# One gradient stored feature-major and turned on its way back, normalised rows turned by SyncE instead of TensorE, layer 2 scheduled later

## The chip, the cores and the metric

The kernel runs on one core of a Trainium2 chip. The metric is the device time of one execution in microseconds (us), as the median of several runs. The engines are named as the profile names them: PE (TensorE, matmuls), DVE (VectorE), ACT (ScalarE), POOL (GpSimd) and SP (SyncE, which here only issues DMAs).

## What is computed

A forward pass of four blocks over x (2048 rows, D = 448 features) and the gradient of its result with respect to eight inputs. Block A is a gated long convolution, block B a two-layer perceptron with F = 1792 hidden features; both are used twice with the same weights.

```
def A(q, k, v, shift_k, ssm_k, ssm_D):
    kv = shift_conv(k, shift_k) * v
    y = causal_conv(kv, ssm_k) + kv * ssm_D        # by FFT of length 4096
    return q * y
def B(x, w1, w2):
    return silu(x @ w1) @ w2
x = A_q
x = x + A(layernorm(x), ...)
x = x + B(layernorm(x), w1, w2)                    # layer 1
x = x + A(layernorm(x), ...)
x = x + B(layernorm(x), w1, w2)                    # layer 2
out, vjp = jax.vjp(all of it);  grads = vjp(grad_out)
```

y does not depend on x, so it is computed once. The gradients of w1 and w2 sum over all 2048 rows and both layers.

## The kernel before, in words

The program has three stages. `Head` computes y by FFT matmuls into the SBUF tile Y. `Flow` then works through 16 tiles of 128 rows. `Tail` computes the weight gradients (its jobs "w2" and "w1") and, by another FFT, the gradients of block A's inputs.

**Order.** Nothing is issued in the order of the source. Every step is a call of `s.op` with an estimated cost for each engine that may do it, the tiles that it reads and writes, and a priority `prio` (smaller is earlier; one unit is about one us). `Sched.plan` plays the steps through with these costs and writes an order for each engine: an engine that is free takes the ready step with the smallest priority for which buffers are free (`_slots`, ring sizes in `BUFS`). `RATE` gives its DMA rates in bytes per us. `emit` then issues the steps in that order. On the chip each engine works strictly in order, and semaphores do the rest.

**A tile** (`Flow.tile(j)`, base priority `b = 20 j`; layer 2 at `c = b + 20`, the gradient of layer 1 at `d = c + 20`):

- x0 is normalised (`norm`: statistics on DVE, a power on POOL, the scaling on DVE), gated (`gate`), giving x1, and normalised again, giving n1.
- n1 must be feature-major for the up-projection. `turn` does four 128x128 transposes on PE into PSUM (L627) and one copy to SBUF, the tile nT, on DVE or ACT (L92, L94).
- `up` (L645, L654, L655) multiplies w1 by nT into two PSUM tiles; `silu` (L673) makes aT and the derivative dT of them on ACT. The two functions need different tables; `TURNED` lists where the derivative comes first.
- `down` (L689) multiplies aT by w2. x2, n2, x3 and n3 follow, then the same for layer 2.
- Backwards, grad_out's tile g is turned by two DMA transposes that SP issues (L757, L758). `grad_up` gives ghT of layer 2 (gh2), `back` and `gate_back` give the tile G2. G2 is turned by `turn` like n1 and n3, and gives gh1 and the gradient of q.

So three turns are done on PE for each tile, 48 in all.

**Stores for the weight gradients.** a1, a2, gh2 and gh1 are feature-major (128 features x 14 x 128 rows); the weight gradients need them row-major. `store_turned` (L676 to L681) has SP issue a DMA transpose into the SBUF tile `turned` (three buffers) and then a plain DMA of it to DRAM: A_d[0], A_d[1], GH_d[1] and GH_d[0]. In `Tail.jobs`, `bring` (L1067 to L1073) loads 256 features of all 16 tiles (1 MB) into a buffer `jb`: three in a ring, and for some loads of "w1" a spare one in the place of Minv, once Minv has been read. PE multiplies `jb` by gmov, G2 or nmov (L1124). The last tile's part of A_d[1] is taken from `turned` itself (`k.lastA`).

Of the kernel before, what the change touches and what calls it, by code (L numbers as in the profile page):

```python
# [13 lines left out]
BF16 = mybir.dt.bfloat16  # L14
ACT = mybir.ActivationFunctionType
ALU = mybir.AluOpType
# [4 lines left out]
P = 128  # L21
S = 2048
D = 448
F = 1792
J = 16
# [107 lines left out]
class Sched:  # L133
# [3 lines left out]
    AHEAD = 0.2  # L137
    STEP = 20
    RATE = {"plain": 300e3, "turn": 160e3}
# [99 lines left out]
    def plan(self):  # L239
# [4 lines left out]
        dma_free = 0.0  # L244
# [103 lines left out]
class Head:  # L348
# [11 lines left out]
    def run(self, pr):  # L360
# [52 lines left out]
        for b in range(4):  # L413
            n = 128 if b < 3 else 64
            for g in range(2):
                pt = s.vb("ps", "d", [P, 8, n], BF16, "ps_kt")

                def tk(e, b=b, g=g, pt=pt, n=n):
                    kv = ksb[b][:].rearrange("p (n1 n2) -> p n2 n1", n2=16)
                    for i in range(8):  # L420
                        nc.tensor.transpose(pt[:, i, :], kv[:, 8 * g + i, :], k.ident[:n, :n])

                s.op({"PE": 0.88}, tk, r=[ksb[b]], w=[pt], prio=pr + 0.1 * b)
                c = n / 128
                s.op({"DVE": 0.07 + 0.54 * c, "ACT": 0.08 + 0.82 * c}, lambda e, b=b, g=g, pt=pt, n=n: _copy(nc, e, kt()[:, 8 * g:8 * g + 8, 128 * b:128 * b + n], pt[:]), r=[pt], w=[kts[b][g]], prio=pr)
# [4 lines left out]
        for jq in range(4):  # L430
            for h in range(2):
                pt = s.vb("ps", "d", [DC, 2, 4, P], BF16, "ps_kT")

                def tt(e, jq=jq, h=h, pt=pt):
                    for u in range(4):
                        for c in range(2):
                            lo = (2 * h + c) * DC
                            nc.tensor.transpose(pt[:, c, u, :], Y.t[:, 4 * jq + u, lo:lo + DC], k.ident[:])

                s.op({"PE": 0.45}, tt, r=k.Yv[4 * jq:4 * jq + 4], w=[pt], prio=pr + 0.2)  # L440
                s.op({"DVE": 0.61, "ACT": 0.9}, lambda e, jq=jq, h=h, pt=pt: _copy(nc, e, kT[h]()[:, jq, :, :, 1:129], pt[:]), r=[pt], w=[kTs[h][jq]], prio=pr + 0.2)
# [3 lines left out]
        for n2 in (*range(1, 16), 0):  # L445
            ps = self.unit([P, 2, 512], name="ps_s1")

            def s1(e, n2=n2, ps=ps):
                for c in range(2):
                    nc.tensor.matmul(ps[:, c, :D], lhsT=M1[:, n2, c, :], rhs=kt()[:, n2, :], start=True, stop=True)  # L450

            s.op({"PE": 0.38}, s1, r=[m1s[n2 // 8], *[x[n2 // 8] for x in kts]], w=[ps], prio=pr, hold=[A1K])
            s.op({"ACT": 0.8, "DVE": 1.0}, lambda e, n2=n2, ps=ps: _copy(nc, e, A1K[:, :, :, n2, :].rearrange("p dh c ds -> p c dh ds"), ps[:, :, :D].rearrange("p c (dh ds) -> p c dh ds", ds=4)),
                 r=[ps], w=[aks[n2]], prio=pr)
# [29 lines left out]
        for ci in range(NCI):  # L484
            turn(A1K, [A1K], Z, zs, ci, pr + 2 + 0.1 * ci)
        for ci in range(NCI):
            stage2(Z, zs, ci, pr + 2 + 0.1 * ci)
# [58 lines left out]
        for h in range(2):  # L546
            for i, jq in enumerate((1, 2, 3, 0)):
                conv(h, jq, pr + 2 + 0.1 * (2 * (4 * h + i)))
# [9 lines left out]
            for ci in range(7 * h, 7 * h + 7):  # L558
                turn(A1v, [avs[ci]], X, xs, ci, pr + 4 + 0.1 * ci - 0.3)
            for ci in range(7 * h, 7 * h + 7):  # L560
                chunk(ci, pr + 4 + 0.1 * ci)
# [4 lines left out]
        for i in range(8):  # L566
# [7 lines left out]
            q = -6 + 0.1 * i if i else -20  # L574
# [5 lines left out]
T_ = 20.0  # L580
EARLY = 2
ROWS = (0, 128, 256, 320)
TURNED = ((1, 0), (1, 1), (3, 0))


class Flow:
# [89 lines left out]
    def store_turned(self, src, dst, j, pr):  # L676
        nc, s = self.nc, self.s
        an = self.small("turned", (P, NF, P))
        self.k.last_turn_out = s.op({"SP": 2.2}, lambda e: nc.sync.dma_start_transpose(out=an[:], in_=src[:].rearrange("p a s -> p (a s)")), r=[src], w=[an], prio=pr, dma=("turn", 458e3))
        s.op({"SP": 0.4}, lambda e: nc.sync.dma_start(out=dst[:, j, :], in_=an[:].rearrange("p a f -> p (a f)")), r=[an], w=[self.k.st_[(id(dst), j)]], prio=pr + 3, dma=("plain", 458e3))  # L680
        return an  # L681
# [42 lines left out]
    def tile(self, j):  # L724
        nc, s, k = self.nc, self.s, self.k
        b = T_ * j
        y = k.Yv[j]
# [7 lines left out]
        self.norm(x0, n0, rs[0], b - 14)  # L735
        self.gate(x0, n0, y, x1, b - 10)
        self.norm(x1, n1, rs[1], b - 8)
        s.op({"POOL": 0.6}, lambda e: nc.gpsimd.dma_start(out=_pm(k.N_d[0][:])[:, j, :], in_=n1[:]), r=[n1], w=[k.st_[("n", 0, j)]], prio=b + 10, dma=("plain", 115e3))
        a1, s1 = self.silu(self.turn(n1, b - 3, "nT1"), 0, b, (j, 0) in TURNED)
        self.store_turned(a1, k.A_d[0], j, b + 4)  # L740
        po = self.down(a1, k.w2, "ps_o", b + 8.6)
        x2, n2, x3, n3 = self.small("x2"), self.small("n2"), self.small("x3"), self.small("n3")
        s.op({"DVE": 0.64}, lambda e: nc.vector.tensor_tensor(out=x2[:], in0=x1[:], in1=po[:, :D], op=ALU.add), r=[x1, po], w=[x2], prio=b + 11)
        self.norm(x2, n2, rs[2], b + 12)
        self.gate(x2, n2, y, x3, b + 16)
        self.norm(x3, n3, rs[3], b + 18)
        s.op({"POOL": 0.6}, lambda e: nc.gpsimd.dma_start(out=_pm(k.N_d[1][:])[:, j, :], in_=n3[:]), r=[n3], w=[k.st_[("n", 1, j)]], prio=b + 35, dma=("plain", 115e3))
        c = b + T_
        a2, s2 = self.silu(self.turn(n3, c + 2.7, "nT3"), 1, c + 5.6, (j, 1) not in TURNED)
        up2 = self.last_up  # L750
        k.lastA = self.store_turned(a2, k.A_d[1], j, c + 10)
        k.lastA_op = k.last_turn_out
# [4 lines left out]
        s.op({"SP": 0.7}, lambda e: nc.sync.dma_start_transpose(out=gT[:, 0:3, :], in_=g[:, 0:384]), r=[g], w=[gT], prio=c - 4, dma=("turn", 98e3))  # L757
        s.op({"SP": 0.4}, lambda e: nc.sync.dma_start_transpose(out=gT[:, 3, :], in_=g[:, 320:448]), r=[g], w=[gT], prio=c - 4, dma=("turn", 33e3))  # L758
        gh2 = self.grad_up(gT, s2, c + 11.3, [up2])
        k.lastG = self.last_up  # L760
        self.store_turned(gh2, k.GH_d[1], j, c + 15)
        po2 = self.down(a2, k.w2, "ps_o", c + 14.2)
# [5 lines left out]
        self.back(gh2, n3, rs[3], g, G3, c + 19.8)  # L768
        s.op({"DVE": 0.32}, lambda e: nc.vector.tensor_tensor(out=gy2[:], in0=G3[:], in1=n2[:], op=ALU.mult), r=[G3, n2], w=[gy2], prio=c + 30)
        self.gate_back(G3, rs[2], y, n2, G2, c + 25)  # L770
# [4 lines left out]
        self.back(gh1, n1, rs[1], G2, G1, d + T_ + 3)  # L775
        gy = self.small("gy")
        q = d + T_ + 8
# [5 lines left out]
    def back(self, gh, n, r, res, out, pr):  # L783
# [4 lines left out]
        s.op({"ACT": 0.85}, lambda e: nc.scalar.activation(u[:], pn[:, :D], ACT.Identity, scale=r[:], accum_out=cp[:, 0:1]), r=[pn, r], w=[u, cp], prio=pr + 3)  # L788
        self.norm_back(u, n, cp, res, out, pr + 4)
# [8 lines left out]
class Tail:  # L798
# [242 lines left out]
    def jobs(self, which, pr):  # L1041
        nc, s, k = self.nc, self.s, self.k
        if which == "w2":
# [4 lines left out]
            groups = [(k.A_d[1], [gs[t // 4] for t in range(NT)], lambda t: gm[:, t, :]), (k.A_d[0], k.G2v, lambda t: k.G2[:, t, :])]  # L1048
        else:
# [7 lines left out]
            groups = [(k.GH_d[1], [nh[1][t // 8] for t in range(NT)], lambda t: nm[1][:, t, :]), (k.GH_d[0], [nh[0][t // 8] for t in range(NT)], lambda t: nm[0][:, t, :])]  # L1057
# [9 lines left out]
        def bring(p, gi, lo, hi, at=None):  # L1067
            b, part, spare = fetch(p, gi, which == "w1" and (2 * p + gi) % 4 == 0)
            src = groups[gi][0]
            v = b.sub()  # L1070
            part[lo:hi] = [v] * (hi - lo)
            k.load = [s.op({"SP": 0.4}, lambda e: nc.sync.dma_start(out=b[:, lo:hi, :], in_=src[:, lo:hi, 256 * p:256 * p + 256]),
                 r=[k.st_[(id(src), j)] for j in range(lo, hi)], w=[v], prio=pr + 12.5 * p + gi if at is None else at, dma=("plain", 65e3 * (hi - lo)), behind=k.load, after=self.done[0] if spare else ())]  # L1073
# [10 lines left out]
        for p in range(NF // 2):  # L1084
            q = pr + 12.5 * p
# [69 lines left out]
def kernel(  # L1155
# [35 lines left out]
    k.A_d = [dram.tile([P, NT, F], BF16, name=f"A_d{i}") for i in range(2)]  # L1191
    k.GH_d = [dram.tile([P, NT, F], BF16, name=f"GH_d{i}") for i in range(2)]
# [26 lines left out]
    "J": dict(jb=3, oo=2),  # L1219
    "S": dict(KK=1, A1K=1, A1v=1, pq=3, skb=1, skc=1),  # L1220
    "E": dict(x0=3, w2T=1, st=2, mv=6, ve=6, n0=5, t1=1, x1=3, n1=5, nT1=1),
    "PM": dict(w2Tr=1, w1T=1, nT3=1, nTg=2, nTG=1, s1=4, T=4, turned=3, x2=1, n2=3, x3=3, n3=3, s2=2, g=3, ghp=2, ob=2,
# [105 lines left out]
```

## Time and profile before

| what | value |
|---|---|
| three runs | 719.62, 720.49 (median), 721.50 us |
| the profiled execution | 722.94 us, of which 721.2 is the span from first to last instruction |
| mean granted PE clock | 0.994 |
| DMA | 160.08 MB, mean 222 GB/s |
| SP's own queue (q1) | 117.85 MB, 66.6% of the 16 DMA engines' span |
| big DMA turns (`turned`) | 64 of 448 KB, median 5.5 us from issue to landing |
| small DMA turns (`nT<-g`) | 32, median 3.2 us |
| stores of `turned` to A_d, GH_d | 64 of 448 KB, median 3.9 and 4.2 us |
| loads `jb` | 28, of 1 MB (two of 960 KB), medians 6.1 to 7.4 us |

In the profile, a line "out<-in" names the written and the read tiles, "L627" is a line of the kernel before, and "x4" counts instructions that are merged. The busy time of PE is modelled, since matmuls are pipelined: the 0.22 us that one 128x128 matmul lasts overlaps with the next ones, and the distance from start to start tells its price. SPq is SP's queue: the time that SP takes to issue a DMA, not the transfer's own.

### The profile page before, as it was taken

The page shows a single profiled execution, that of the slowest core. Times are in us where ns is not written, and L with a number is a line of the kernel's source. Part 1 is how long each engine was busy: PE and PEld are TensorE (multiplying, and loading weights), DVE is VectorE, ACT ScalarE, POOL GpSimd, SP SyncE. Part 2 cuts the span into 40 slices and gives each one's busy share as a digit, 9 for nine tenths or more (in the row PEclk, how much of TensorE's full clock was granted, in tenths as well). Part 3 has the DMA queues.
Part 4 walks back from the last instruction along what each step waited for, and adds up shares of the span by engine and source line. Part 5 has one row for each costly group of instructions (what it writes and reads, how often), then busy time and mean ns, then how long its engine had stood idle before and what let it go on. Part 6 is the DMA issues. An engine that isn't in the chain of part 4 may idle for free. (4 is left out here: it accounts for less than half of the span.)

```text
span 721.2 us, 18320 instructions
## 1 busy us (share of the span) xinstructions
PE 695.1 (96%) x7664; PEld 484.8 (67%) x7664; DVE 516.7 (72%) x1215; ACT 419.8 (58%) x518; POOL 158.9 (22%) x266
## 2 busy tenths in 40 slices
PE   6999879999999999999999999999999999999997
PEld 5887657777777777777777776655576766555553
DVE  4989775669988889888988867671479857959100
ACT  4899876586667765776667755521676555111311
POOL 1244153112321233222321211003123203100000
PEclk9999998999999999999999999999999999999999
DMA  9989988899889898888878798979759949996751
GB/s 323 275 236 291 344 143 179 183 217 210 190 187 190 213 202 179 190 208 226 167 181 188 205 213 200 305 217 280 214 181 370 319 139 329 354 292 191 193 130 27
DMA packets 230720, 160.08 MB, mean 222 GB/s; under 512 B 145326, under 2 KB 207966, under 8 KB 230252
## 3 DMA queue, kind: packets, MB, share of 16 engines
q1 hardware_dynamic: 216862, 117.85, 66.6%
q0 software_dynamic: 13008, 40.24, 17.3%
q8 instruction: 60, 0.98, 0.6%
q10 hardware_dynamic: 766, 0.80, 0.3%
q14 instruction: 24, 0.20, 0.1%
HBM read 65.36 MB, written 54.60 MB: 166 GB/s over the span
## 5 line engine op out<-in xcount | busy, mean ns | idle before, releaser
L1124 PEld LDWEIGHTS <-jb 128*128 128x128 bf16 x892 | 85.7, 98 | 77.8 <-DMA jb<-GH_d 1.2
L645 PE MATMUL ps_h<-nT,w1sb 128*128 128x128 bf16 x1344 | 88.0, 222 | 5.7 <-DVE nT L94 4.9
L689 PE MATMUL ps_n<-w1T,ghT 128*128 128x448 bf16 x448 | 90.0, 352 | 1.4 <-ACT u L788 0.9
L689 PE MATMUL ps_o<-w2sb,aT 128*128 128x448 bf16 x448 | 90.1, 353 | 0.0
L645 PEld LDWEIGHTS <-w1sb 128*128 128x128 bf16 x1344 | 79.4, 99 | 14.5 <-DVE nT L94 4.8
L1124 PE MATMUL ps_d<-nmov,jb 128*128 128x448 bf16 x448 | 87.9, 353 | 0.8 <-DMA jb<-GH_d 0.8
L645 PE MATMUL ps_g<-nT,w2T 128*128 128x128 bf16 x1344 | 85.8, 219 | 0.7 <-ACT nT L92 0.7
L645 PEld LDWEIGHTS <-w2T 128*128 128x128 bf16 x1344 | 77.3, 98 | 7.4 <-issue 0.8
L701 ACT CAST ghp<-ps_g 128x896 bf16<-128x896 f32 x64 | 57.9, 907 | 39.0 <-PE ps_g L654 22.5
L673 ACT ACTIVATE aT<-ps_h 128x896 bf16<-128x896 f32 x64 | 56.9, 916 | 26.3 <-PE ps_h L654 19.7
L689 PEld LDWEIGHTS <-ghT 128*128 128x128 bf16 x448 | 42.6, 98 | 37.3 <-issue 1.8
L689 PEld LDWEIGHTS <-aT 128*128 128x128 bf16 x448 | 42.6, 98 | 35.1
L713 DVE SCALAR_TENSOR_TENSOR junk<-u,n 128x448 bf16<-128x448 bf16 x64 | 39.9, 623 | 32.5 <-ACT u L788 31.8
L673 ACT ACTIVATE dT<-ps_h 128x896 bf16<-128x896 f32 x64 | 57.1, 917 | 8.8 <-PE ps_h L645 5.3
L610 POOL TENSOR_TENSOR rstd<-ve,mhalf 128x1 f32<-128x1 f32 x64 | 45.5, 711 | 55.0 <-DVE ve L607 52.9
L1124 PE MATMUL ps_d<-G,jb 128*128 128x448 bf16 x224 | 45.5, 352 | 0.0
L1124 PE MATMUL ps_d<-gmov,jb 128*128 128x448 bf16 x220 | 45.0, 352 | 0.0
L673 ACT ACT_TABLE_LOAD x34 | 43.6, 1283 | 0.6
L92 ACT CAST dob<-ps_d 128x448 bf16<-128x448 f32 x14 | 7.5, 533 | 59.8 <-PE ps_d L1124 59.8
L702 DVE TENSOR_TENSOR ghT<-ghp,dT 128x896 bf16<-128x896 bf16 x64 | 38.5, 622 | 4.8 <-ACT ghp L701 4.8
L788 ACT ACTIVATE u<-ps_n,rstd 128x448 bf16<-128x448 f32 x32 | 20.4, 637 | 36.7 <-PE ps_n L689 36.7
L605 DVE BATCH_NORM_STATS2 st<-x 128x6 f32<-128x448 bf16 x64 | 39.9, 624 | 1.2
(174 smaller groups left out, 1258.4 us busy)
## 6 DMA issues: line engine op xcount, KB each, us to landing
A_d<-turned SPq DMA_DIRECT2D x32, 448.0 KB, 3.9
GH_d<-turned SPq DMA_DIRECT2D x32, 448.0 KB, 4.2
jb<-GH_d SPq DMA_DIRECT2D x14, 1024.0 KB, 7.2
jb<-A_d SPq DMA_DIRECT2D x12, 1024.0 KB, 7.4
KK<-KK POOLq DMA_DIRECT2D x14, 256.0 KB, 5.4
spec_K<-KK POOLq DMA_DIRECT2D x7, 512.0 KB, 6.5
spec_KV<-X POOLq DMA_DIRECT2D x7, 512.0 KB, 12.3
N_d<-n POOLq DMA_DIRECT2D x32, 112.0 KB, 3.6
```

What stands on the lines that cost most here:

```text
L92: nc.scalar.copy(out, in_)
L605: nc.vector.bn_stats(out=st[:], in_=x[:])
L610: s.op({"POOL": 1.0}, lambda e: nc.gpsimd.tensor_tensor(out=rs[:], in0=ve[:], in1=self.k.mhalf[:, 0:1], op=ALU.pow), r=[ve], w=[rs], prio=pr)
L645: nc.tensor.matmul(ps[:, i, :], lhsT=at(b, ft), rhs=nT[:, b, :], **f)
L673: prev = [s.op({"ACT": 0.93}, lambda e, i=i, fun=fun, out=out: nc.scalar.activation(out[:, 7 * i:7 * i + 7, :], h[i][:], fun), r=[h[i]], w ...
L689: nc.tensor.matmul(po[:, :D], lhsT=a[:, ft, :], rhs=wt[:, ft * D:(ft + 1) * D], start=(ft == 0), stop=(ft == NF - 1))
L701: s.op({"ACT": 0.93}, lambda e, i=i, t=t: nc.scalar.copy(t[:], G[i][:]), r=[G[i]], w=[t], prio=pr)
L702: s.op({"DVE": 0.57}, lambda e, i=i, t=t: nc.vector.tensor_tensor(out=gh[:, 7 * i:7 * i + 7, :], in0=t[:], in1=d[:, 7 * i:7 * i + 7, :], o ...
L713: nc.vector.scalar_tensor_tensor(out=junk[:], in0=u[:], scalar=1.0, in1=n[:], op0=ALU.mult, op1=ALU.mult, accum_out=cp[:, 1:2])
L788: s.op({"ACT": 0.85}, lambda e: nc.scalar.activation(u[:], pn[:, :D], ACT.Identity, scale=r[:], accum_out=cp[:, 0:1]), r=[pn, r], w=[u, cp ...
L1124: nc.tensor.matmul(ps[:, :D], lhsT=rows(t, gi, u), rhs=at(t), start=(first and t == ts[0]), stop=(last and t == ts[-1]))
```

## The change

1. **Layer 2's gradient (gh2) is stored as it is**, feature-major, into a DRAM tensor [1792, 2048] named GH1, by one DMA issued from SP (`store`, with `RAW = ("GH1",)`). Each contiguous piece has 128 elements, 256 bytes. The seven loads of it in the job "w1" are DMA transposes from DRAM. a1, a2 and gh1 are stored as before (named A0, A1 and GH0).
2. **Turns by SP.** 38 of the 48 turns become two DMA transposes each, issued by SP, like those of g. The ten in `ON_PE`, in the first and last tiles, stay on PE.
3. **Layer 2 and the gradient of layer 1 get later priorities**: `c = b + 20 + 8.2`, `d = c + 20 + 7.9` (`SKEW`).
4. **Single steps** get a priority of their own (`NUDGE`, read by `s.at`), the list `TURNED` grows from three entries to nine, and in `back` the matmuls can have another priority than the steps after them (`px`).
5. The planner's DMA model keeps a time for each issuing queue beside the common one. `turned` has two buffers instead of three, nT3 and nTG two instead of one. lastA is a small DMA transpose of its own (131 KB).

```diff
-    RATE = {"plain": 300e3, "turn": 160e3}
+    SHARED = 3.0
+    RATE = {"plain": 300e3, "turn": 160e3, "load": 190e3, "rows": 220e3}
...
+    def at(self, base, *key):
+        return base + NUDGE.get(key, 0.0)
...
-                        dma_free = max(dma_free, o.end) + nbytes / self.RATE[kind]
-                        o.end = dma_free + 1.8
+                        took = nbytes / self.RATE[kind]
+                        dma_all = max(dma_all, o.end) + took
+                        dma_free[e] = max(dma_free[e], o.end) + took
+                        o.end = max(dma_free[e], dma_all - self.SHARED) + 1.8
...
-TURNED = ((1, 0), (1, 1), (3, 0))
+SKEW = (8.2, 7.9)
+TURNED = ((0, 1), (1, 0), (1, 1), (3, 0), (4, 1), (13, 1), (14, 0), (14, 1), (15, 0))
+NUDGE = {(8, "ch"): 0.3, (3, "h1"): -16, (14, "h2"): -2, (4, "iy"): 0.3, (4, "n2"): 6, (1, "o1"): 2, (3, "o2"): 18, (14, "t3"): -16, (4, "tG"): -2, (8, "tk"): 2.4, (6, "tt"): -1, (9, "tv"): -0.3, (11, "tv"): -1, (13, "tv"): 0.1, (2, "x1"): 10}
+RAW = ("GH1",)
+ON_PE = ((0, 0), (0, 1), (1, 0), (2, 0), (2, 2), (4, 2), (14, 1), (14, 2), (15, 1), (15, 2))
...
-    def turn(self, src, pr, tag, after=()):
+    def turn(self, src, pr, tag, on_pe, after=()):
         nc, k, s = self.nc, self.k, self.s
+        if not on_pe:
+            nT = self.small(tag, (P, ND, P))
+            nT.name = "nT"
+            s.op({"SP": 1.2}, lambda e: nc.sync.dma_start_transpose(out=nT[:, 0:3, :], in_=src[:, 0:384]), r=[src], w=[nT], prio=pr - EARLY, dma=("turn", 98e3))
+            s.op({"SP": 1.2}, lambda e: nc.sync.dma_start_transpose(out=nT[:, 3, :], in_=src[:, 320:448]), r=[src], w=[nT], prio=pr - EARLY, dma=("turn", 33e3))
+            return nT
...
+    def store(self, src, nm, j, pr):
+        nc, s, k = self.nc, self.s, self.k
+        dst = k.rows_d[nm]
+        if nm not in RAW:
+            self.store_turned(src, nm, j, pr)
+            return
+        at = dst.rearrange("(a p) s -> p a s", p=P)[:, :, P * j:P * j + P]
+        s.op({"SP": 0.45}, lambda e: nc.sync.dma_start(out=at, in_=src[:]), r=[src], w=[k.st_[(nm, j)]], prio=pr, dma=("rows", 458e3))
...
-        c = b + T_
+        c = b + T_ + SKEW[0]
...
-        d = c + T_
+        d = c + T_ + SKEW[1]
-        gh1 = self.grad_up(self.turn(G2, d + 14, "nTG"), s1, d + 16.9)
-        self.store_turned(gh1, k.GH_d[0], j, d + 20)
+        gh1 = self.grad_up(self.turn(G2, at("tG", d + 14), "nTG", (j, 2) in ON_PE), s1, at("gG", d + 16.9))
+        self.store(gh1, "GH0", j, d + 20)
...
+            if nm in RAW:
+                cost, kind, get = 0.3 * n, "load", lambda e: nc.sync.dma_start_transpose(out=b[:, lo:hi, :], in_=src[fs, P * lo:P * hi])
+            else:
+                cost, kind, get = 0.4, "plain", lambda e: nc.sync.dma_start(out=b[:, lo:hi, :], in_=src[:, lo:hi, fs])
```

More of the change, by code (lines that the diff above doesn't have):

```diff
@@ L740, in tile @@
-        self.store_turned(a1, k.A_d[0], j, b + 4)
-        po = self.down(a1, k.w2, "ps_o", b + 8.6)
+        a1, s1 = self.silu(self.turn(n1, at("t1", b - 3), "nT1", (j, 0) in ON_PE), 0, at("h1", b), (j, 0) in TURNED)
+        self.store(a1, "A0", j, b + 4)
+        po = self.down(a1, k.w2, "ps_o", at("o1", b + 8.6))
         x2, n2, x3, n3 = self.small("x2"), self.small("n2"), self.small("x3"), self.small("n3")
-        s.op({"DVE": 0.64}, lambda e: nc.vector.tensor_tensor(out=x2[:], in0=x1[:], in1=po[:, :D], op=ALU.add), r=[x1, po], w=[x2], prio=b + 11)
@@ L749, in tile @@
-        a2, s2 = self.silu(self.turn(n3, c + 2.7, "nT3"), 1, c + 5.6, (j, 1) not in TURNED)
+        c = b + T_ + SKEW[0]
+        a2, s2 = self.silu(self.turn(n3, at("t3", c + 2.7), "nT3", (j, 1) in ON_PE), 1, at("h2", c + 5.6), (j, 1) not in TURNED)
         up2 = self.last_up
-        k.lastA = self.store_turned(a2, k.A_d[1], j, c + 10)
-        k.lastA_op = k.last_turn_out
+        if j == NT - 1:
+            k.lastA = s.vb("J", "lastA", [P, 4, P], BF16, "lastA")
+            k.lastA_op = s.op({"SP": 1.2}, lambda e: nc.sync.dma_start_transpose(out=k.lastA[:], in_=a2[:, 0:4, :].rearrange("p a s -> p (a s)")), r=[a2], w=[k.lastA], prio=c + 10, dma=("turn", 131e3))
@@ L753, in tile @@
+        self.store(a2, "A1", j, c + 10)
         g = self.small("g")
@@ L1056, in jobs @@
                          r=[k.st_[("n", i, j)] for j in range(8 * h, 8 * h + 8)], w=[nh[i][h]], after=self.done[i], prio=pr - 30 if i else pr + 0.5, dma=("plain", 917e3))
[L1057 removed]
+            groups = [("GH1", [nh[1][t // 8] for t in range(NT)], lambda t: nm[1][:, t, :]), ("GH0", [nh[0][t // 8] for t in range(NT)], lambda t: nm[0][:, t, :])]
         out7 = k.outs[7].rearrange("(c p) f -> p c f", p=DC)
@@ L1190 @@
     k.N_d = [dram.tile([S, D], BF16, name=f"N_d{i}") for i in range(2)]
-    k.A_d = [dram.tile([P, NT, F], BF16, name=f"A_d{i}") for i in range(2)]
-    k.GH_d = [dram.tile([P, NT, F], BF16, name=f"GH_d{i}") for i in range(2)]
+    k.rows_d = {nm: dram.tile([F, S] if nm in RAW else [P, NT, F], BF16, name=f"{nm}_d") for nm in ("A0", "A1", "GH0", "GH1")}
     bf = mybir.dt.np(BF16)
```

90 lines of the change are left out of this document (46 added, 44 removed).

## The prediction

> **What bounds the kernel now.** I read the page first (busy shares and slices), then the windows, the waits of TensorE, the chain in order of time, and SyncE's timeline.
>
> ```profile
> span 721.2 us, 18320 instructions
> PE 695.1 (96%) x7664; PEld 484.8 (67%) x7664; DVE 516.7 (72%) x1215; ACT 419.8 (58%) x518; POOL 158.9 (22%) x266
> ...
> 160.00:440.00 280.00, 280.00 (x3541) 207.64 (x3539) 243.72 (x701) 190.58 (x243) 72.91 (x113) 1.00 0.85 194
> ```
>
> The third line is a window (start:end, its length, then busy time of PE, PEld, DVE, ACT and POOL, the granted clock, the DMA share, GB/s). Through the steady tiles TensorE has no idle time at all, at full clock, while DVE has 13% free, ACT 32% and the DMA engines 15%. So here an instruction less on PE shortens the span, and one less elsewhere does not. A PE busy share alone would not prove that matmuls run back to back; the timeline of PE does:
>
> ```profile
> 302.21 0.39 PE L627 MATMUL ps_t<-ident,n 128*128 128x128 bf16 x4
> 302.43 1.34 PE L645 MATMUL ps_g<-nT,w2T 128*128 128x128 bf16 x21
> ...
> 310.98 0.39 PE L627 MATMUL ps_t<-ident,n 128*128 128x128 bf16 x4
> 311.20 1.11 PE L689 MATMUL ps_n<-w1T,ghT 128*128 128x448 bf16 x5
> ```
>
> A turn of a normalised tile is four transposes; the next matmul starts 0.22 us after the turn did (0.39 is the pipelined length of the four). Where PE does wait, the list of its waits and the windows tell:
>
> ```profile
> PE ps_h L645 <- DVE nT L94: 4.9, 2, 3.7
> ...
> PE ps_d L1124 <- DMA jb<-GH_d: 0.8, 1, 0.8
> ...
> 100.00:120.00 20.00, 16.29 (x186) 12.64 (x184) 9.05 (x26) 12.53 (x14) 5.39 (x11) 0.83 1.02 165
> ...
> 440.00:480.00 40.00, 37.59 (x407) 25.41 (x406) 29.08 (x81) 16.87 (x23) 3.89 (x7) 1.00 1.12 294
> ```
>
> The ramp (100 to 120) loses 3.7 us in one wait, and runs some time at a lower granted clock (0.83 mean). The drain (440 to 480) loses 2.4 us in four waits. One load of GH_d costs 0.8 us.
>
> **The change, part by part.**
>
> *Turns taken off PE.* Of 48 turns, 10 stay on PE (ON_PE: the first and the last tiles). 38 go. Each costs 4 transposes, 0.22 us from start to start: 38 x 0.22 = 8.4 us. In the order of the built program the steady tile keeps its 56 + 56 + 56 + 56 up-projection matmuls and its four down-projections, so nothing is added on PE. The tile's period is 23.05 us now (SyncE's rows at 304.46 and 327.51) and would be 23.05 - 3 x 0.22 = 22.4. Taken: -8.4. The 38 copies out of PSUM (587 ns on ACT, 421 on DVE) hide behind PE already: 0.
>
> *The same turns on SyncE.* Each becomes two DMA issues. This is the load to watch, for SyncE issues in order; one tile of now:
>
> ```profile
> 304.46 1.12 SPq L680 DMA_DIRECT2D A_d<-turned  x1
> 308.24 1.79 SPq L679 DMA_TRANSPOSE turned<-ghT  x1
> 310.08 1.29 SPq L680 DMA_DIRECT2D GH_d<-turned  x1
> 312.12 2.38 SPq L679 DMA_TRANSPOSE turned<-aT  x1
> 314.85 0.40 SPq L680 DMA_DIRECT2D GH_d<-turned  x1
> 317.72 0.32 SPq L680 DMA_DIRECT2D A_d<-turned  x1
> 320.98 1.31 SPq L679 DMA_TRANSPOSE turned<-aT  x1
> 322.81 1.74 SPq L757 DMA_TRANSPOSE nT<-g  x1
> 324.60 1.23 SPq L758 DMA_TRANSPOSE nT<-g  x1
> 325.92 1.54 SPq L679 DMA_TRANSPOSE turned<-ghT  x1
> ```
>
> Four big turns 7.0 us, four stores 3.1, one turn of g 3.0: 13.1 of 23.05. Afterwards: three big turns 5.3, three stores 2.4, one feature-major store of GH1, and four small turns (g and the three moved ones) 4 x 3.0 = 11.9. The new store has no row; it is an issue of 1792 pieces of 256 bytes. Nearest rows: a jb load of 2048 pieces issues in 0.52 us (median), a turn of the same tile in 1.8. With 0.08 us between issues (1.0 for 13), the sum is 21.1 to 22.4 of a period of 22.4. So SyncE would be 94 to 100% booked. Behind a late issue stand the next turns, and behind these PE. I walked one tile in the built order: n1's turn, the A0 store between its halves, gh1's turn, G2, a2's turn, n3, the GH0 and GH1 stores, g, the A1 store, a1's turn; 21 us from n1 being ready, and n1 of the next tile is ready 22.4 later. The shortest cover is n1's: ready about 8 us of PE work ahead of its up-projection, of which 4 are issues and 3.2 the landing (nT<-g, x32). G2 and n3 have over 5 us to spare; that is what the two skews (8.2 and 7.9) buy. The skews also move layer 2's stores, its N_d and out_0 stores on POOL's queue and the loads of g by as much; these queues have room (POOL is 22% busy), and nothing on the path reads what they store. I take +0.6 for single late turns; the ends are 0 and the sum of the third rival.
>
> *GH1 stored feature-major.* It saves a big turn (5.5 us to land) and the wait of its store on it, and nobody reads GH1 for 200 us or more: 0 on PE. DMA time: one turn (5.5) and one store (4.2) less, one store in small pieces and three pairs of small turns (3.2 per issue) more; about even, at a share of 0.85 now, 0.88 in the shorter period. The row: 448 KB in 256-byte pieces lands in 5.5 us, in 3584-byte rows in 4.2. The Trainium skill, "DMA: Bandwidth & Descriptors", Specifications, asks for at least 512 bytes for line rate, and says that below it the engine reads, modifies and writes. By that rule the new store would cost about twice 4.2 us of landing instead of 5.5; no run here shows it yet. Such a store would feed the third rival below.
>
> *GH1 turned by the w1 loads.* Seven loads of 1 MB become turns. Nearest row: w1T, 784 KB turned from DRAM, lands 7.2 to 9.7 us after issue; a plain 1 MB jb load 7.2. So 9.4 to 12.7 each. A step of this stage takes 12.5 us of PE (6.05 + 0.22, twice, in the chain). The ring of four buffers gives a load 12.5 to 15.5 us before it is read: covered, by 0 to 6 us. At the start of the stage the engines are full (share 1.11 in 620 to 640, and the 0.8 us wait), but the built order puts 19 us of PE work instead of 12.5 between the last read of Minv, which frees the first buffer, and the first use of what is loaded there. Taken 0; ends -0.8 and +3.5. The Trainium skill, "Advanced Engine Details and Errata", X-Bar Transpose, holds turns to be as fast as plain DMAs; the rows differ (784 KB in 7.2 to 9.7 against 1024 KB in 7.2), and by that rule this term would be 0 without the bounds.
>
> *Ramp.* PE's order is unchanged up to the fourth up-projection, and DVE still stands through the same chain of 5 us before the copy that PE waits 3.7 us for. 0, ends -2 and +2 (the clock may fall elsewhere). *Drain.* Between the last tile's down-projection and the turn of its G2, PE has 5.5 us of other work instead of 4.5, and three of the four waits lose their turn or get this cover: -1.2; ends -2.4 and +2. *Head and tail FFT, nudges, the order of Silu and its derivative, lastA, buffer counts:* single steps among the same neighbours; PE waits there under 2 us in all for anything but loads: 0, ends -2 and +2. POOL keeps its issues (22% busy).
>
> Sum: -8.4 + 0.6 - 1.2 = -9.0. Against the profiled execution: span 721.2 to 712.2, and with the 1.7 around it 722.9 to 713.9. The median shown is 720.49, 2.4 below that execution; so I forecast 720.49 - 9.0 = **711.5**.
>
> **Rivals.**
>
> 1. *SyncE lags a little* (period 22.7 to 23.0, not 22.4): 13 tiles give back 4 to 8 us, 716 to 719. For it: the 94 to 100% above. Against: most of the 3.0 of a small turn follows a big one; early turns took 1.20 + 1.24.
> 2. *Nothing is gained*, since another engine holds the tile: DVE has 20.1 us of work in 23.05 and a chain through ACT and POOL. PE's full windows speak against it. About 720.
> 3. *SyncE and its DMA rings set the period* (the other side). If the small pieces back up the rings, the three big turns take what the slowest of the steady tiles takes (2.94 at 279.84 us, instead of 1.8) and the new store 1.8: 21.1 + 3.4 + 1.3 = 25.8, the dear end. It decides from 23.05 on, where the tile is longer than today. In the middle, at 23.5, 13 tiles x 0.45 = 6 more than now, less 1.2 from the drain: 725; at the dear end 13 x 2.75 = 36: 755. By the 512-byte rule of the Trainium skill this is what would happen first.
> 4. *The turned loads bind the w1 stage*: 12.7 of landing plus 3 of queueing behind the plain load is 15.7 a step, against 12.5: 3.2 x 5 steps = +16, less 9: 727.
>
> Chances: forecast 0.60 (708 to 715), rival 1 0.15, rival 2 0.07, rival 3 0.14, rival 4 0.04. About 0.3% (2.2 us) is what a measurement can tell from no change. Faster holds the forecast and most of rival 1: 0.73; same 0.10; slower 0.17. The range leaves rivals 3 and 4 out: 707.5 to 722.5.
>
> **What would show it.** The steady window should keep PE at 20 of 20 with a distance of 22.4 between tiles; PE waits named nT from a DMA would show rival 1 or 3, with SyncE's rows without a gap; a wait of ps_d on jb from GH1 shows rival 4. The ramp's 3.7 us wait on the DVE copy should still stand. I am wrong if the new store's issue takes over 2 us, or if the landing of nT goes from 3.2 to over 6.

## The result, and the profile after

The changed kernel takes **737.15 us** in the median (736.6 to 737.4), the kernel before 720.06 beside it: 1.022 of the time before, interval 1.020 to 1.024. So it is 17 us slower, where 9 us less was forecast. The profiled execution took 737.32 us. Its page, then its windows, to be read like those of before:

```profile
span 735.5 us, 18095 instructions
...
PE 692.0 (94%) x7495; PEld 478.9 (65%) x7512; DVE 510.0 (69%) x1201; ACT 409.5 (56%) x496; POOL 154.9 (21%) x266
```

```profile
100.00:120.00 20.00, 15.86 (x181) 12.34 (x183) 8.96 (x25) 13.62 (x15) 4.97 (x9) 0.83 0.79 165
160.00:440.00 280.00, 270.35 (x3305) 196.82 (x3304) 232.10 (x672) 175.07 (x216) 66.70 (x110) 0.99 0.87 187
440.00:480.00 40.00, 39.57 (x474) 28.35 (x471) 33.06 (x93) 18.94 (x28) 3.83 (x7) 1.00 1.04 273
600.00:660.00 60.00, 52.37 (x481) 27.86 (x480) 40.10 (x79) 8.18 (x12) 6.97 (x12) 0.94 1.02 247
```

The second of these four windows is the news: PE was busy 280 of 280 us in the steady tiles, and is now idle for 9.65 of them. The last one is the start of the job "w1": 58.97 of 60 before, 52.37 now, at a granted clock of 0.94. The ramp stands as it was, the drain is better. At the top of the list of PE's waits stand one that is new (nT by DMA) and one that was 0.8 us (jb):

```profile
PE ps_h L661 <- DMA nT<-n: 9.6, 7, 4.3
PE ps_d L1157 <- DMA jb<-GH_d: 6.3, 3, 4.0
PE ps_h L661 <- DVE nT L94: 5.9, 3, 3.7
```

**Where the time went.** I took PE's distances from start to start. The usual (median) distance of each operation is its work, a granted clock of one half adds to that, and the rest is idle time (small pauses of 0.05 us between groups are in it, in both kernels). In the trace of the changed kernel 17 records of matmuls are missing (7495 of PE beside 7512 weight loads; 11 in the head, 6 in the transforms of the tail). They are counted here as work of 0.216 us each, or 3.7 us would pass for idle time.

| us | before | after | difference | predicted |
|---|---|---|---|---|
| work of PE | 664.4 | 656.2 | -8.2 | -8.4 |
| tiles, 140 to 440: idle | 10.7 | 21.7 | +11.0 | +0.6 |
| tiles: half clock | 0 | 2.7 | +2.7 | 0 |
| drain, 440 to 500 | 4.1 | 1.9 | -2.2 | -1.2 |
| start of w1, 600 to 660: idle | 4.8 | 11.8 | +7.0 | 0 |
| start of w1: half clock | 0 | 2.5 | +2.5 | 0 |
| head, to 100 | 13.9 | 14.9 | +1.0 | 0 |
| transforms of the tail, 500 to 600 | 3.4 | 4.6 | +1.2 | 0 |

With the ramp (-0.3), the end (+0.3) and the time ahead of PE's first matmul and behind its last (-0.5) that is +14.5, and the spans differ by 14.3. (The medians differ by 17.1: the profiled execution of before lay 2.9 us above its median.)

**One wait in the tiles, followed back.** PE's timeline, then SP's queue ahead of it:

```profile
265.52 0.28 PE L661 MATMUL ps_h<-nT,w1sb 128*128 128x128 bf16 x2
267.89 1.22 PE L661 MATMUL ps_h<-nT,w1sb 128*128 128x128 bf16 x19 [2.10 <-DMA nT<-n]
```

```profile
254.51 1.23 SPq L635 DMA_TRANSPOSE nT<-G  x1
255.83 1.55 SPq L705 DMA_TRANSPOSE turned<-aT  x1
257.43 1.75 SPq L634 DMA_TRANSPOSE nT<-n  x1
259.23 0.81 SPq L706 DMA_DIRECT2D GH_d<-turned  x1
260.14 0.40 SPq L699 DMA_DIRECT2D GH_d<-ghT  x1
260.58 3.08 SPq L635 DMA_TRANSPOSE nT<-n  x1
263.75 1.20 SPq L785 DMA_TRANSPOSE nT<-g  x1
```

`up` multiplies blocks 0, 1 and 3 of nT first. PE did two matmuls (x2) and then stood for block 3, the second of the two turns. That one left SP 3.15 us after the first, with two stores in between; its own issue took 3.08, and it landed 4.2 us after that. SP has no pause in these rows. Between 140 and 440 SP is busy 261 of 300 us (179 before), and another 13 lie in pauses of under 0.2 us between issues: 91% booked. Small turns of n take 1.58 and 1.91 us in the mean to issue, from 1.1 up to 3.3; big turns of aT 2.16. The new store issues in 0.51.

The 3.08 us are not the small turn's own. Between 140 and 440, 27 of the 32 small turns right behind another small turn issue in 1.20 to 1.25 us, and those right behind a plain store in 1.1 to 2.7. All 12 that stand right behind the new feature-major store take 2.0 to 3.3, and 2.8 or more in the nine cases where, as here, a plain store stands ahead of that one. So the store is cheap to issue, and the issue behind it pays. Of the seven waits on nT<-n, three (2.10, 0.75 and 0.30 us) have these two stores between the halves of the turn. In three others (4.28, 1.35 and 0.55 us) SP had itself stood, ahead of the late half, for 0.7 to 3.1 us, until a big turn had landed that a store waits for.

**The start of w1.** SP's queue after, and then before:

```profile
611.07 19.59 SPq L1100 DMA_TRANSPOSE jb<-GH_d  x2
630.75 1.01 SPq L1083 DMA_DIRECT2D nmov<-N_d  x2
631.85 10.20 SPq L1102 DMA_DIRECT2D jb<-GH_d  x2
```

```profile
609.53 5.73 SPq L1072 DMA_DIRECT2D jb<-GH_d  x2
615.35 5.11 SPq L1055 DMA_DIRECT2D nmov<-N_d  x2
620.55 21.73 SPq L1072 DMA_DIRECT2D jb<-GH_d  x5
```

The first two turned loads hold SP for 19.6 us, the two plain ones held it for 5.7. What stands behind them, the two halves of N_d[0] and GH0, goes out 11 to 15 us later than before, where PE comes to this stage 8 us later (628.8, before 620.8). PE waits twice:

```profile
637.58 4.71 PE L1157 MATMUL ps_d<-nmov,jb 128*128 128x448 bf16 x24 [1.89 <-DMA jb<-GH_d]
646.33 5.68 PE L1157 MATMUL ps_d<-nmov,jb 128*128 128x448 bf16 x16 [4.03 <-DMA jb<-GH_d]
```

The first wait ends as the second turned load itself lands (637.53), which left SP 7.8 us after the first; the second ends as a load of GH0 lands (646.28) that stood behind both. From 660 on no step waits for a load. The kernel before had shown what turned loads take to issue, in two rows of w1T in its head:

```profile
87.21 4.60 SPq L1277 DMA_TRANSPOSE w1T<-in_B_w_dram  x1
101.18 7.15 SPq L1277 DMA_TRANSPOSE w1T<-in_B_w_dram  x1
```

### The profile page after: what moved, and what is told of

The parts are those of the page before. It is cut to its first block, busy times and chain, and to the rows that moved or that the text cites. A ratio compares the mean times of both kernels' runs of the same rounds, so it can differ in the third digit from the quotient of the medians.

```text
span 735.5 us, 18095 instructions
## 1 busy us (share of the span) xinstructions
PE 692.0 (94%) x7495; PEld 478.9 (65%) x7512; DVE 510.0 (69%) x1201; ACT 409.5 (56%) x496; POOL 154.9 (21%) x266
## 5 line engine op out<-in xcount | busy, mean ns | idle before, releaser
L661 PE MATMUL ps_h<-nT,w1sb 128*128 128x128 bf16 x1344 | 91.2, 225 | 15.6 <-DMA nT<-n 9.6
L1157 PE MATMUL ps_d<-nmov,jb 128*128 128x448 bf16 x448 | 90.2, 359 | 6.3 <-DMA jb<-GH_d 6.3
L620 POOL TENSOR_TENSOR rstd<-ve,mhalf 128x1 f32<-128x1 f32 x64 | 41.9, 656 | 92.1 <-DVE ve L617 92.0
```

The lines of the kernel that those rows point to most:

```text
L620: s.op({"POOL": 1.0}, lambda e: nc.gpsimd.tensor_tensor(out=rs[:], in0=ve[:], in1=self.k.mhalf[:, 0:1], op=ALU.pow), r=[ve], w=[rs], prio=pr)
L661: nc.tensor.matmul(ps[:, i, :], lhsT=at(b, ft), rhs=nT[:, b, :], **f)
L1157: nc.tensor.matmul(ps[:, :D], lhsT=rows(t, gi, u), rhs=at(t), start=(first and t == ts[0]), stop=(last and t == ts[-1]))
```

## The experiments

The theory: SP, which issues in order, is the bottleneck at two places. In the tiles the small turns queue behind other issues (the queue theory); at the start of w1 the turned loads block what is behind them (the load theory). The rivals: the 256-byte store loads the DMA engines (the pieces or DMA theory); the moved layer 2 and the single placements cost time by themselves. Differences below are of the ratios to the kernel before, times 720. "Planned anew" means that the planner made another order; "order kept" means that only what an issue does, or its queue, was edited.

### GH1 by rows again (planned anew)

```diff
-RAW = ("GH1",)
+RAW = ()
```

> The changed kernel with GH1 stored row by row as before (a big turn and a plain store in each tile; plain loads in the w1 stage). Queue theory (SyncE's in-order queue is full in the steady tiles, and the turned loads hold it at the start of the w1 stage): the tile gets one turn of 1.6 to 2.2 us and one store of 0.6 for a store of 0.5, so about 2 us more on a queue that is 91% booked; with 13 steady tiles the steady part gets 5 to 25 us longer and the start of the w1 stage 9 us shorter: 733 to 753 us, with more nT waits from DMA than the 9.6 us of the changed kernel. Pieces theory (the 256-byte store loads the DMA engines and delays the small turns): the nT waits go, 737 - 14 - 9 = 714 us. Under both, the 6.3 us wait of ps_d on jb goes back to about 1.

Measured: 749.95 us, ratio 1.040 (1.036 to 1.043), 13 us over the changed kernel. The pieces theory, which asked for 714, falls as the whole account; the delay of the issue behind the feature-major store, shown above, is not tested by this run, which puts a big turn and a plain store in its place. The waits don't all have the name that I expected: 7.4 us for nT by DMA, but 10.3 for ghT, whose tile waits for its big turn, and SP itself stands 15 us for `turned` to be stored (two buffers, for four big turns a tile again). Waits on jb are no longer in the list.

### All turns on PE again (planned anew)

```diff
+ON_PE = tuple((j, i) for j in range(16) for i in range(3))
```

> The changed kernel with all 48 turns of normalised rows on TensorE as before; GH1 stays feature-major and its loads stay turned. Queue theory: SyncE's load falls by some 9 us a tile, the waits of the steady tiles go (-14), TensorE does 38 turns more (+8.4), the 9 us at the start of the w1 stage stay: 731 us. Theory that the moved layer 2 and the single placements cost the steady tiles: the idle time stays, 737 + 8.4 = 745. Pieces theory: nT no longer comes by DMA, so the waits go too, 731; told from the queue theory by the run with rows.

Measured: 732.65, ratio 1.016 (1.013 to 1.019). The number is the queue theory's, and from 260 to 440 PE has no wait at all. But 6 us of idle time are left between 140 and 260, so the number alone proves little.

### The second small turn left out (order kept)

```diff
-nc.sync.dma_start_transpose(out=nT[:, 3, :], in_=src[:, 320:448])
+nc.gpsimd.memset(nT[:, 3, :], 0.0)
```

> The changed kernel with its written order kept; of each normalised row that SyncE turns, only the first three blocks are turned, and the fourth is set to zero by GpSimd (that part of the computation is left out). SyncE loses 38 issues of 1.2 to 1.9 us, the DMA engines only 33 KB each. Queue theory (SyncE's time is what the tiles wait for): the nT waits and the clock dips behind them go, -11 to -14: 723 to 726. DMA theory (bytes in flight, not issues): bytes fall by under 2 per cent, the waits stay: 735 to 737.

Measured: 721.53, ratio 0.9997 (0.997 to 1.003), 16 us under the changed kernel. Its window of the tiles, and then rows of one down-projection in three kernels (before, this one, the changed one), each with its next tile's:

```profile
160.00:440.00 280.00, 280.00 (x3505) 204.78 (x3503) 243.09 (x699) 182.03 (x226) 75.03 (x145) 1.00 0.86 194
```

```profile
253.45 2.81 PE L689 MATMUL ps_o<-w2sb,aT 128*128 128x448 bf16 x14
...
276.50 2.81 PE L689 MATMUL ps_o<-w2sb,aT 128*128 128x448 bf16 x14
```

```profile
258.27 2.81 PE L714 MATMUL ps_o<-w2sb,aT 128*128 128x448 bf16 x14
...
280.65 2.81 PE L714 MATMUL ps_o<-w2sb,aT 128*128 128x448 bf16 x14
```

```profile
259.93 2.81 PE L714 MATMUL ps_o<-w2sb,aT 128*128 128x448 bf16 x14
...
286.15 2.81 PE L714 MATMUL ps_o<-w2sb,aT 128*128 128x448 bf16 x14
```

The tile takes 23.05 us before, 22.38 here and 26.2 in the changed kernel (24.7 in the mean of its six tiles from 236 to 385). So the gain of 0.67 a tile exists, 3 x 0.22, and 38 issues of 33 KB each decide whether it is seen. The bytes are the same within 1%. With the issue its landing goes too, and so does the issue behind the feature-major store; that it is a matter of SP's queue is shown by this run together with the next two. Of the 20 us between the two profiled executions 13.3 lie in the tiles, and 5.9 at the start of w1, which the edit does not touch.

### The plain stores on GpSimd's queue (order kept)

```diff
-nc.sync.dma_start(out=dst[:, j, :], ...)
+nc.gpsimd.dma_start(out=dst[:, j, :], ...)
```

> The changed kernel with its written order kept; the plain stores of the turned tiles (A0, A1, GH0) are issued from GpSimd's queue instead of SyncE's. SyncE loses 3 issues of 0.6 us a tile and, more, the places where a store stands in front of a turn. Queue theory: half of the 14 us or more comes back, 724 to 731, unless GpSimd, which then waits for each turn to land before its next power step, holds the normalisation. DMA theory: 737. If GpSimd's waits cost more than they free: above 740, with PE waits that name POOL's rows.

Measured: 730.35, ratio 1.011 (1.008 to 1.015): 8 us back, as the queue theory had it. PE's idle time between 140 and 440 falls from 9.65 to 4.10 us. The same edit on the plan of the next run did the opposite (below).

### True issue times in the plan (planned anew)

```diff
-s.op({"SP": 1.2}, ... nT[:, 0:3, :]   # and 1.2 for nT[:, 3, :], 0.7 and 0.4 for g
+s.op({"SP": 1.7}, ... nT[:, 0:3, :]   # and 1.9, 1.6 and 1.6
-cost, kind, get = 0.3 * n, "load", ...   # a plain store 0.4
+cost, kind, get = 0.6 * n, "load", ...   # a plain store 0.7
```

> The changed kernel, planned with the issue times that its trace shows (a small turn 1.6 to 1.9 us instead of 1.2, or 0.7 and 0.4 for g; a plain store 0.7 instead of 0.4; a turned load twice as long). If the cost in the tiles comes from a plan that thinks SyncE has a third less to do than it has: better placed issues, 724 to 731. If SyncE is too full in any order (21 of 22.4 us): no gain, 735 to 750, with other places of waiting.

Measured: 724.67, ratio 1.004 (1.002 to 1.007), 13 us under the changed kernel. The same work on the same queue, which is now busy even for 277 of the 300 us (261 in the changed kernel), with its issues in another order:

```profile
160.00:440.00 280.00, 275.58 (x3430) 200.76 (x3429) 237.23 (x685) 179.14 (x222) 68.28 (x113) 1.00 0.88 191
```

```profile
257.83 1.33 SPq L634 DMA_TRANSPOSE nT<-n  x1
259.21 1.39 SPq L635 DMA_TRANSPOSE nT<-n  x1
260.64 0.58 SPq L706 DMA_DIRECT2D A_d<-turned  x1
```

In these rows the two halves of a turn stand together, and the store comes after them. The wait of the tiles is 4.4 us instead of 9.65, and the start of w1 has 58.87 of 60 us busy. So SP isn't too full for any order; it was too full for an order that was planned with too little time for each issue. The drain pays 4 us for it: 35.56 of 40 busy, 39.57 in the changed kernel, with waits for gmov, which is loaded there.

### Stores on GpSimd's queue in that plan (order kept)

The same edit as above, on the kernel with true issue times.

> The plan with the issue times of the trace, its order kept, and the plain stores of the turned tiles on GpSimd's queue. Queue theory: of the 6 us of idle time left in the tiles (280 to 440) half goes, 720 to 723. If GpSimd's waits for the turns hold the normalisation: 725 to 728.

Measured: 735.18, ratio 1.018 (1.014 to 1.022): 10 us worse than without it. In its profiled execution (730.8) PE waits 8.6 us for the turned G2 (five times), and GpSimd stands for big turns ahead of stores. That fits the price named in the expectation, but it is not shown; what moving the stores brings depends on the plan.

### GH1 loaded without turning (order kept)

This kernel leaves the turn of GH1 out.

```diff
-dma_start_transpose(out=b[:, lo:hi, :], in_=src[fs, P * lo:P * hi])
+dma_start(out=b[:, lo:hi, :], in_=src[fs, P * lo:P * hi].rearrange("(p u) (t c) -> p (u t) c", u=2, c=256))
```

> The changed kernel with its written order kept; the seven loads of GH1 in the w1 stage are plain copies of the same bytes (not turned, so the gradient of w1 is left wrong). If the turned loads cost the start of the w1 stage: -7 to -10, 727 to 730, and the waits of ps_d on jb fall to about 1 us as before. If the stage starts late for another reason (the moved order, N0 waiting for its buffer): the waits stay, 735 to 737; the run with both parts undone, 13 us over the time before with 3.5 us of such waits left, speaks for some of this.

Measured: 725.88, ratio 1.007 (1.004 to 1.009): 11 us back. The waits on jb are no longer in the list, and the first two loads leave SP free at once (0.32 us of issue each; the first row has a pause of 1.9 between them):

```profile
611.92 2.50 SPq L1100 DMA_DIRECT2D jb<-GH_d  x2
614.51 1.28 SPq L1083 DMA_DIRECT2D nmov<-N_d  x2
622.49 7.24 SPq L1102 DMA_DIRECT2D jb<-GH_d  x2
```

### N0 and the first GH0 loads on GpSimd's queue (order kept)

```diff
-nc.sync.dma_start(out=nm[i]...), nc.sync.dma_start(out=b...)
+(nc.sync if i else nc.gpsimd).dma_start(out=nm[i]...), (nc.gpsimd if which == "w1" and p < 2 else nc.sync).dma_start(out=b...)
```

> The changed kernel with its written order kept; at the start of the w1 stage the loads of N0 and the first two loads of GH0 are issued from GpSimd's queue, so that they don't stand behind the two turned loads. If SyncE's queue, held for 19.6 us by the two turned loads, is the cost: the 4.0 and 1.9 us waits of ps_d on jb and the clock dip behind them go, -6 to -9: 728 to 731. If the turned loads themselves land late (their own transfer, or the DMA engines full): no change, 736 to 738, or the waits move to the loads of GH1.

Measured: 750.4 in two executions of four (the others took 762 and 764), ratio 1.040 (1.037 to 1.043). A miss, and the second branch of the expectation: the waits move to the turned loads of GH1. PE's two long waits, and the second turned load:

```profile
625.84 3.05 PE L1157 MATMUL ps_d<-nmov,jb 128*128 128x448 bf16 x8 [6.99 <-DMA jb<-GH_d]
654.77 5.44 PE L1157 MATMUL ps_d<-nmov,jb 128*128 128x448 bf16 x16 [20.68 <-DMA jb<-GH_d]
```

```profile
608.91 35.80 SPq L1100 DMA_TRANSPOSE jb<-GH_d  x1
```

Both waits end as one of SP's first two turned loads lands (625.79 and 654.72). Beside the loads that GpSimd issues, the second of these holds SP for 35.8 us (11.8 in the changed kernel), and GpSimd's own two loads of jb take 22 and 27 us to land, where those that SP issues later take 6.5. So it is not enough to take the plain loads off SP's queue: with all of them under way together, the turned loads themselves come late.

### The two halves of w1 exchanged (planned anew, the tiles unchanged)

```diff
-groups = [("GH1", ... nm[1]), ("GH0", ... nm[0])]
+groups = [("GH0", ... nm[0]), ("GH1", ... nm[1])]   # N0 loaded first, buffers exchanged too
```

> The changed kernel with the two halves of the w1 job exchanged: the plain loads of GH0 and N0 come first and are multiplied first, the turned loads of GH1 second. Everything up to the w1 stage keeps its written order. Load theory (two turned loads at the start hold SyncE's queue for 19.6 us, and what they hold and they themselves come late): with some 12 us of TensorE's work ahead of the first turned bytes, 6 to 9 of the 9 us at the start of the stage come back: 728 to 731. If any order of these 6 MB is too late at that place, because the DMA engines are full: 735 to 738.

Measured: 727.62, ratio 1.009 (1.006 to 1.012): 9 us back, nearly all that the start of w1 had lost (idle from 600 to 660: 7.0 us, before 4.8, changed kernel 11.8; no half clock).

```profile
610.81 4.57 SPq L1083 DMA_DIRECT2D nmov<-N_d  x2
615.48 0.70 SPq L1102 DMA_DIRECT2D jb<-GH_d  x1
620.81 16.75 SPq L1100 DMA_TRANSPOSE jb<-GH_d  x2
```

Two turned loads still hold SP for 16.75 us, but now nothing urgent is behind them. With the run that loads GH1 without turning, this shows the load theory: the turned loads at the head of the stage are the cost there, and their place in the order decides it. How much is what they hold up (a wait of 4.03 us in the changed kernel) and how much their own lateness (1.89 and 0.36), these runs don't separate.

### Both together, and a turn back on PE

The exchange with the stores on GpSimd's queue:

> The exchange in the w1 job and the plain stores of the turned tiles on GpSimd's queue together. If the two costs are separate places, the gains add: 730 with the stores moved, less 6 to 9: 721 to 724. If the gain of the moved stores was only shifted into the w1 stage (the profile of that run shows 10 us of idle time there, 4 of them more than in the changed kernel), up to 12 us come back: 718.

Measured: 721.13, ratio 0.999 (0.997 to 1.002). The two gains add: equal to the kernel before.

The exchange, and n1's turn of tiles 3 to 13 on PE (`ON_PE = ON_PE + tuple((j, 0) for j in range(3, 14))`, planned anew):

> The exchange in the w1 job, and n1's turn of tiles 3 to 13 back on TensorE (11 turns); n3 and G2 of these tiles stay with SyncE, the plan is made anew, stores stay on SyncE. Queue theory: SyncE loses about 3 us of its 21 a tile, and the turn with the shortest cover is no longer behind it: the steady waits go (-14), TensorE does 11 x 0.22 = 2.4 more, the exchange gives 8: 717, faster than the kernel before. If the moved layer 2 and the plan cost the tiles by themselves, as the run with both parts undone suggests for the first tiles (8 us of idle time between 120 and 240): 722 to 727.

Measured: 723.59, ratio 1.002 (0.999 to 1.004): 6.6 us over the queue theory's number. 5.7 us of waits are left in the tiles, and a dip of the clock.

All three:

> The three together: the exchange in the w1 job, the plain stores of the turned tiles on GpSimd's queue, and n1's turn of tiles 3 to 13 on TensorE. Queue theory: the plan is that of the run with n1 on TensorE, and of its 7.5 us of idle time between 120 and 400 and its one clock dip most go, as 3 to 5 of the 11 in the changed kernel's tiles did with the stores moved: 724 less 4 to 8, so 716 to 720, faster than the kernel before or equal to it. If what is left there does not come from SyncE's queue, or GpSimd's longer waits delay the normalisation: 723 to 726.

Measured: 724.93, ratio 1.006 (1.003 to 1.008). A miss: the tiles improve a little, but GpSimd's queue puts new waits on the normalisation (PE ps_t <- DVE n, 1.5 us). No version here beats the kernel before.

### What is left with both parts undone

Both undone (`RAW = ()`, `ON_PE` all), the rest of the change kept; then also `SKEW = (0.0, 0.0)`; then also `NUDGE = {}` and the old `TURNED`; then also the old DMA model of the planner. And `NUDGE = {}` alone in the changed kernel. All planned anew.

> Both back: turns on TensorE and GH1 by rows; what is left of the change is the moved layer 2, the single placements, the list TURNED and the buffer counts. If the two queue costs are all: the time before, 720, plus the 3 us of the head and 2 us of the tail transforms that the trace shows besides, so 720 to 725. If the moved layer 2 costs by itself: 730 or more.

> Turns on TensorE, GH1 by rows, and layer 2 and the gradient of layer 1 back at their old priorities (SKEW 0); the single placements stay. If the later layer 2 is what costs the 13 us that were left with both parts undone: 720 to 724. If the single placements, made for another plan, are it: 730 to 740.

> As the run before it, and without the single placements and with the old list TURNED: what is left of the change is the planner's DMA model, the buffer counts (turned 2 instead of 3) and lastA. If these are neutral, as predicted: 719 to 723. If the two buffers or the model cost something: 725 or more, with waits for buffers of turned.

> As the run with only the rest of the change (turns on TensorE, GH1 by rows, old priorities, no single placements), and the planner's DMA model as it was before; what is left is the two buffers of turned, the second buffer of nT3 and of the turned g's and G2's tiles, and lastA as a small turn of its own. If the planner's new DMA model is what costs the 12 us that were left: 719 to 723. If the buffers or lastA are: 728 or more.

> The changed kernel without the single placements (the list NUDGE empty). If they are responsible for the 3.2 us in the head and 2.3 in the transforms of the tail: 732. If they are neutral, as predicted: 737 within 2. If the plan of the tiles leans on them: above 740.

Measured: 734.01 (ratio 1.017, 1.014 to 1.021), 735.34 (1.020, 1.017 to 1.023), 733.10 (1.018, 1.012 to 1.025), 741.67 (1.029, 1.026 to 1.032) and 752.33 (1.042, 1.035 to 1.048). None comes back to 720. The later layer 2 is not the reason, for without it the 13 us stay; nor is it one cause: the first has 5.5 us of waits in the tiles, the third 4 us more in the head, the fourth a single wait of 10.4 us on jb at the start of w1 (its loads of GH go out at 627 instead of 610). A new plan shifts the time by up to 15 us, and the single placements fit one plan: without them the changed kernel is 14 us slower. One rival stands untested here: in all four kernels with both parts undone `turned` has two buffers for four big turns a tile, where the kernel before has three. SP stands 28 to 45 us in them until a store has freed a buffer of `turned`, and not at all in the kernel before. In the fourth, the buffer counts and lastA are, besides the plan, all that is left of the change, and it is 21 us slower than the kernel before. How much of that the third buffer would give back, no run shows. So a part's worth can't be read from a run that was planned anew; the runs with the order kept carry the verdicts above.

The plan with true issue times, the old DMA model and no single placements in the head:

> The changed kernel planned with the issue times of its trace, with the old DMA model and without the single placements in the head (those of the tiles stay). If the new model costs the head and the tail 5 us or more: 716 to 720, under the 724.7 of the plan with true issue times alone. If the new model is what placed the turns well in the tiles: 725 or more.

Measured: 727.09, ratio 1.010 (1.006 to 1.014). The head is that of before again (idle time from 40 to 100: 9.2 us, before 9.2, changed kernel 10.4), so the new model with its placements costs the 1.2 us there; the start of w1 loses more than that, in a wait of 4.5 us for a load of jb.

## Why the prediction was wrong

1. **Turns off PE, -8.4: right.** 22.38 against 22.4 for the tile, where nothing else waits; -8.2 of PE's work in all.
2. **SyncE, "I take +0.6 for single late turns": the step that failed.** It cost 13.7 (11.0 idle, 2.7 half clock). The load was estimated well: 94 to 100% forecast, 91% measured. What failed is the walk through a tile with mean issue times. It named "the A0 store between its halves" and still gave each turn its mean. On the chip one small issue takes 1.1 to 3.3 us, and PE waits for the half that comes last, behind whatever the plan put in front of it. Rival 1 had this mechanism, at 4 to 8 us and a chance of 0.15: half the size. Rival 3's point (a tile beyond 23.05) was passed, and a part of its reason is in the rows: the new store issues in 0.51 us, not 1.8, but a small turn right behind it takes 0.8 to 2.1 us more than behind another small turn. The run with GH1 by rows, with a fourth big turn instead, is slower still, so the store's share of the 13.7 stays open. My signs of being wrong stayed silent: they named the store's own issue (0.51) and the landing of nT, which is 3.4 in the median, but 5.5, 7.3 and 7.7 in the three waits where the turn stands behind that store. That the plan gave SyncE 1.2 us where the chip takes 1.6 to 1.9 stood in the diff beside the rows, and I used the rows without asking what order the planner would make of its own number. With true times its plan came out 13 us shorter on the same, still fuller queue: not the booked share decided, but which issue stood ahead of which.
3. **Turned loads, "Taken 0; ends -0.8 and +3.5": failed too**, at +9.5. I priced the landing of each load (9.4 to 12.7 forecast; 6.2 to 18.7, median 8.2), and looked for its reader. The price was the 19.6 us in which two of them hold SP's queue, and its payers the second of them and GH0 behind both. The prediction's own nearest rows, of w1T in the kernel before, had an issue of 4.6 and one of 7.2 us (shown above) beside the landing that was used. The rule on moved steps, to name what is queued behind, would have found it. Rival 4 (each step bound) is false: from 660 on nothing waits. The Trainium skill, "Advanced Engine Details and Errata", X-Bar Transpose, holds turns to be as fast as plain DMAs. Here the median landing is 8.2 us, against 6.3 for the same seven loads unturned; the issue takes 4.1 to 11.8 us, against 0.3 to 1.1.
4. **GH1's store, 0: not shown to be 0.** It lands later (4.7 us, 3.0 for GH0's plain one), and nothing waited for its bytes. But the issue behind it pays, and three of the seven waits on nT (3.1 us in all) end in such an issue. The Trainium skill, "DMA: Bandwidth & Descriptors", Specifications, asks for at least 512 bytes; here the 256-byte pieces took 1.6 times as long to land as the plain store, where the prediction made about twice of that rule.
5. **Ramp 0: right. Drain -1.2: right in sign, -2.2. Head and transforms 0: a little low**, +1.0 and +1.2, each inside the ends of 2 us; for the head the planner's model with its placements is shown, for the transforms nothing is. Why both parts undone don't give back 720 stays open beyond what is said above.

## What to carry to other kernels

Work that is moved from a full engine to a queue that issues in order costs its place in that queue: price each urgent issue by what stands ahead of it, at the longest issue times and not the mean, and each issue made longer by what stands behind it. An issue that looks cheap can make the one behind it dear. Exchanging two groups of loads was worth 9 us here, and telling the planner the measured issue times 13. Where a planner makes the order, judge a part of a change by runs that keep the order, for a new plan alone shifted the time by up to 15 us.

## What the runs showed of the hardware

- Two turned loads of 1 MB held the issuing queue for 16.8 to 19.6 us; the same bytes unturned were issued within 2.5. A plain load is not always quick to issue: 0.5 us in the median, and 9.6 and 9.8 behind other loads (SP at 632.50 in the changed kernel, at 621.16 before).
- A small turn of 33 KB takes as long to issue as one of 98 KB (1.91 and 1.58 us in the mean, about 1.2 at the least for either). What stands ahead sets it: 1.2 us behind another small turn, 2.0 to 3.3 right behind a store of 448 KB in 256-byte pieces, whose own issue took 0.5.
- Two loads of jb that GpSimd issued beside two turned loads of SP landed in 22 and 27 us, and one of the turned loads took 35.8 us to issue.
- A wait of 2.10 us on PE (above) was followed by 3.4 us at half the granted clock; waits of 1.35 and 1.89 us in the same execution were not. The Trainium skill, "TensorE: Matmul & The Clock Gate", Part 1, gives at least one idle window of about 3.4 us for that; here a shorter wait was enough. Not every longer wait did it: one of 3.4 us in the run with the second turn left out did not.
